# Weight loads beside attention's first loads, a one-piece softmax for the third half sequence, and new ranks for the first stage

## The chip, the cores and the metric

The kernel runs on one core of one Trainium2 chip. The metric is the device time of one execution in microseconds (us); the time before is the median of three runs. All rows of traces come from one profiled execution of the kernel before.

## What is computed

Eight batches of windowed attention over eight heads (576 positions, 64 wide), the heads side by side as rows of a 4608 x 512 matrix, and a feed-forward layer with an exact gelu on it, in float32:

```
scores = q @ k.T / 8
scores = where(mask, scores, -1e9)   # heads 0-3: the last 32 keys
                                     # heads 4-7: every 4th of the last 128 keys
attn = exp(scores - max(scores))
attn = attn / (sum(attn) + 1e-9)
x = (attn @ v) rearranged to [4608, 512]
h = x @ w_in                         # 512 -> 2048
g = 0.5 * h * (1 + erf(h / sqrt(2)))
out = g @ w_out                      # 2048 -> 512
```

The two weight matrices come as float64 (the kernel gets them as pairs of 32-bit words and makes a high and a low float32r part of each number).

## The kernel before

The 4608 rows are cut into 16 half sequences of 288 rows, `c` = 0 to 15. Attention of one half sequence is done for four pairs of heads, `p` = 0 to 3: pairs 0 and 1 have the plain window (96 rows in use), pairs 2 and 3 the dilated one (128 rows). "(1,3)" below is half sequence 1, pair 3.

For each pair `load` (L271) fetches queries and keys, `load_v` (L280) the values, `scores` (L302) multiplies queries and keys on PE, `lowest` (L318) adds the mask and finds the lowest of the negated scores on DVE, in three steps of two instructions, `softmax` (L331) takes the exponential on ACT, in three steps of two instructions of 64 columns each, with the row's lowest as bias and the row's sum as a second result. `norm` (L338) divides by the sum (two small DVE instructions and one multiplication of 128 x 384), `turn` (L351) transposes, `av` (L363) multiplies with the values on PE, and `xout` splits the product into a high part (ACT) and a low part (DVE), `xh` and `xl`.

The feed-forward layer runs over 16 blocks `f` of the hidden dimension. `ffn_h` (L410) makes 12 matmuls of 128 x 288 for one block and half sequence, then the gelu and a cast on ACT and a subtraction on DVE (L426). `ffn_o` (L428) makes 12 matmuls per block for the output. Each block needs the weights `win[f]` and `wouts[f]`. A weight block of 128 x 512 float64 numbers is fetched by `w_load` (L193), one transfer of 512 KB, and split by `w_rest` and `w_low`: six DVE instructions of 128 x 512 (L241, L243, L203, L205, L209, L253) and one cast on ACT. Block 0 of `w_in` takes another way, `w_join` and `w_join_pe`, with three matmuls on PE.

There are two stages. In the second, the half sequences 2 to 15 go one after the other in an order written by hand (from L573 on): feed-forward of `c`, with the attention of `c + 1` put between its matmuls. The first stage does everything else: all 32 weight blocks, attention of half sequences 0, 1 and 2, and the feed-forward layer of 0 and 1. Here a planner (`Plan`, L49) sets the order. Each piece of work is a job with costs in us, a list of jobs that it follows, buffers that it takes and gives back, and a rank. The planner keeps a clock per engine, and takes at each step the job that could start first, with a small weight of the rank (`KAPPA`); the constants at L39 to L46 are its margins and ranks. Its result is only the order in which instructions stand in each engine's queue: on the chip each engine works through its queue in order and waits at an instruction whose inputs are not there.

What matters for the change: SP issues all transfers, in its own order. `weight_jobs` (L508) starts the first weight load only after the last of the query/key loads of half sequence 0 has begun, and lets at most five weight blocks be loaded ahead of the splitting. Gelu and exponential need different tables of ACT, so all exponentials of half sequence 1 come before the first gelu, and those of half sequence 2 behind the last gelu of half sequence 1 (`gate`, L534). The values of half sequence 2 use the buffer of half sequence 1's `x` parts, and are loaded once that is free. Output blocks `d` = 2 and 3 of half sequence 1 are left for the end of the first stage (96 matmuls), to give PE work while the third softmax runs. Below, h(c,f) is `ffn_h` of half sequence `c` and block `f`; h(2,0) is the first work of the second stage.

Of the kernel before, what the change touches and what calls it, by code (L numbers as in the profile page):

```python
# [12 lines left out]
ALU = mybir.AluOpType  # L13
# [24 lines left out]

LATE, LATE_PE, COLD = 0.25, 0.2, 45  # L39
KAPPA, AHEAD, N_PE = 5.4e-05, 5, 1  # L40
R_ATT, R_P = (0, 340, 260), -12
R_F = 220
R_A = {"load": 152, "v": -162, "scores": -118,
       "exp": 52, "norm": 28, "t": -206, "av": 2, "x": -288, "low": -58}
R_W, R_WL = -76, 1092
R_H, R_O, R_E, R_O1 = 1088, 976, 780, 544  # L46

# [84 lines left out]
def attn_ffn(ctx: ExitStack, tc: tile.TileContext, qk_p, qk_d, v_p, v_d, w_in, w_out, outT):  # L132
# [60 lines left out]
    def w_load(s, src, dst, i):  # L193
        yield {"DMA": 1.6}
        s["raw"] = wo.tile([P, DM, 2], U32, tag="wo", name="raw_w")
        nc.sync.dma_start(s["raw"], src.bitcast(U32).rearrange("p (n t) -> p n t", t=2))
# [167 lines left out]
    def av(s, banks=None):  # L364

        yield {"PE": (0.9 if s.plain else 1.2) if s.c < 2 else 0.9}
        n = NU * s.nq
# [105 lines left out]
    def attention_jobs(plan, c, prev, gate):  # L473

        for p in range(NPAIR):
# [19 lines left out]
            def all_of(name, n):  # L495
                return [(name,) + k] + [(name, u) + k for u in range(n - 1)]
            add("scores", scores(s), [("load",) + k] + [("scores",) + j for j in last], ["m", "m"], [ring])
            chained("low", NU, lowest, lambda b: [("scores",) + k], ["sm"], ["m", "m"])
            chained("exp", NU, softmax, lambda b: [all_of("low", NU)[0] if b == NU - 1 else ("low", b) + k] + gate)
            add("norm", norm(s), all_of("exp", NU))  # L500
            add("t", turn(s), [("norm",) + k], ["sm"], ["sm"])
            own = ["px"] if c < 2 else ["m", "m"]
            add("av", av(s), [("t",) + k, v], own, ["sm"] + ([ring] if c < 2 else []))
            add("x", xout(s), [("av",) + k] + ([("x1",)] if c == 1 else [("h", 0, NF - 1)] if c == 2 else []), give=own)
# [3 lines left out]
    def weight_jobs(plan, i):  # L508
# [6 lines left out]
        def add(name, gen, after, take=(), give=(), delay=0.15):  # L515
            plan.add((name, i), gen, after, take, give, rank + (R_WL if name == "wload" else 0), delay)
        chain = ([("begun", ("wload", i - 1))] if i else [("begun", ("load", 0, NPAIR - 1))])
        if i >= AHEAD:
# [14 lines left out]
    k = attention_jobs(plan, 1, k, [])  # L533
    attention_jobs(plan, 2, k, [("h", 1, NF - 1)])  # L534
    plan.add(("units",), w_units(), take=["go"], rank=R_W)
    for i in range(2 * NF):
# [9 lines left out]
    for f in range(NF):  # L546
        rank = R_W + R_F * f
        for c, gs in ((0, g0), (1, g1)):
            plan.add(("h", c, f), ffn_h(xs[c], f, gs), [("x", c, p) for p in range(NPAIR)] +
                     [("wlow", 2 * f), ("whigh", 2 * f)] + [("exp", 1, p) for p in range(NPAIR)] +  # L550
                     ([("begun", ("h", c, f - 1))] if f else []),
# [133 lines left out]
```

## Time and profile before

| | us |
|---|---|
| median of three runs | 969.88 |
| the runs | 967.44, 969.88, 969.89 |
| the profiled execution | 969.69 |
| its span, first to last instruction | 967.9 |
| PE busy / DVE busy / ACT busy in the span | 931.8 / 486.4 / 439.0 |
| h(0,0) starts on PE | 50.62 |
| h(2,0) starts on PE | 173.96 |

The span is cut by stages. From 0 to 40 us the transfers run at 89% of what 16 DMA engines can be busy, and PE is busy for 16 us of 40. From 40 to 141 us DVE is busy without a gap, mostly with the splitting of weights. From 141 to 174 us the first stage ends, and from 174 us on PE is busy all the time, in equal pieces of 56.9 us per half sequence. A busy share over the whole span (PE 96%) says little here; the stages have to be read one by one.

### The profile page before, as it was taken

To read this page: it belongs to the slowest core of one execution; us is meant where nothing else is said; L and a number is where in the kernel's file an instruction comes from. 1 tells how busy PE (TensorE), PEld (TensorE's weight loads), DVE (VectorE), ACT (ScalarE), POOL (GpSimd) and SP (SyncE) were. 2 spreads that over 40 slices of the span, in tenths; PEclk is the share of its full clock that TensorE was granted. 3 is DMA by queue.
4 is the path that set the end of the run, shared out by engine and by line. 5 is a ranking of instruction groups with operands and counts; after the bars stand their busy time and mean duration, and the time that the engine had idled before them with its cause. 6 is when DMAs were issued, how large, how long until landed. Compare 5 with 4: busy or idle time off the path is not lost.

```text
span 967.9 us, 27863 instructions
## 1 busy us (share of the span) xinstructions
PE 931.8 (96%) x11860; PEld 910.6 (94%) x11860; DVE 486.4 (50%) x1796; ACT 439.0 (45%) x1420; POOL 5.6 (1%) x27
## 2 busy tenths in 40 slices
PE   3689989999999999999999999999999999999998
PEld 3489988999999999999999999999999999999998
DVE  4699996353354535335353533536353363624420
ACT  5445445462634546263454625345362544536240
POOL 2000000000000000000000000000000000000000
PEclk9999999999999999999999999999999999999999
DMA  9633323304021130402203040220404022040000
GB/s 304 247 132 105 114 88 109 130 8 142 2 87 64 46 104 8 142 2 78 73 26 124 8 142 2 78 72 14 136 7 140 4 77 73 8 142 8 20 1 25
DMA packets 32252, 74.80 MB, mean 77 GB/s; under 512 B 3584, under 2 KB 11776, under 8 KB 32128
## 3 DMA queue, kind: packets, MB, share of 16 engines
q1 hardware_dynamic: 32128, 73.02, 22.8%
q8 instruction: 93, 1.52, 0.7%
q14 instruction: 31, 0.25, 0.1%
HBM read 63.57 MB, written 9.44 MB: 75 GB/s over the span
## 4 chain that ended last, share of the span: by engine, by line
PE 86%; DVE 9%; DMA 3%; issue 1%; ACT 0%; SPq 0%; DVEq 0%
PE ps_o L431 39%; PE ps_h L417 38%; PE px_a L386 4%; PE ps_a L315 3%; DVE cv L205 2%; DVE raw_w L243 2%; DMA raw_qk<-qk_p 1%; PE px L386 1%; DVE g L426 1%; DVE raw_w L209 1%; DVE cv L203 1%; DVE win L253 1%; DVE wout L253 1%; DVE raw_w L241 1%; DMA raw_qk<-qk_d 1%
## 5 line engine op out<-in xcount | busy, mean ns | idle before, releaser
L431 PE MATMUL ps_o<-g,wout 128*128 128x288 f32 x3072 | 425.3, 297 | 2.4 <-DVE g L426 1.4
L431 PEld LDWEIGHTS ps_o<-g,wout 128*128 128x128 f32 x3072 | 412.9, 189 | 4.9 <-DVE g L426 2.3
L417 PE MATMUL ps_h<-xh,win 128*128 128x288 f32 x1920 | 391.1, 298 | 3.0 <-DVE win L253 1.7
L417 PEld LDWEIGHTS ps_h<-xh,win 128*128 128x128 f32 x1920 | 309.0, 188 | 6.8 <-DVE win L253 2.5
L417 PE MATMUL ps_h<-xl,win 128*128 128x288 f32 x960 | 283.4, 295 | 0.0
L426 DVE TENSOR_TENSOR g<-gf,g 128x288 fp32r<-128x288 f32 x256 | 117.1, 458 | 260.2 <-ACT g L424 260.1
L421 ACT ACTIVATE gf<-ps_h 128x288 f32<-128x288 f32 x256 | 105.2, 411 | 299.6 <-PE ps_h L417 298.8
L417 PEld LDWEIGHTS ps_h<-xl,win 128*128 128x128 f32 x960 | 181.5, 189 | 0.0
L335 ACT ACTIVATE sm<-sm,st 128x64 f32<-128x64 f32 (+1 forms) x384 | 127.8, 334 | 11.3 <-DVE st L327 11.1
L424 ACT CAST g<-gf 128x288 fp32r<-128x288 f32 x256 | 110.9, 433 | 7.8
L404 ACT CAST xh<-px_a 128x288 fp32r<-128x288 f32 x52 | 28.0, 539 | 140.7 <-PE px_a L386 112.1
L362 DVE STREAM_TRANSPOSE turned<-sm 32x192 f32<-32x192 f32 x196 | 72.4, 369 | 5.2
L335 ACT ACTIVATION_READ_ACCUMULATOR sm<-sm,st 128x1 f32 (+1 forms) x384 | 71.8, 187 | 0.0
L181 DVE COPY o_sb<-ps_o 128x288 f32<-128x288 f32 x61 | 27.7, 455 | 86.7 <-PE ps_o L431 82.2
L406 DVE TENSOR_TENSOR xl<-px_a,xh 128x288 fp32r<-128x288 f32 x52 | 29.6, 569 | 58.4 <-ACT xh L404 58.0
L327 DVE CUSTOM_DVE_ANT_0 sm<-ps_a,masks 96x64 f32<-96x64 f32 (+1 forms) x312 | 46.9, 217 | 0.0
L386 PEld LDWEIGHTS px_a<-turned,v_all 64*64 64x64 f32 x2184 | 38.6, 134 | 4.2 <-issue 4.2
L386 PE MATMUL px_a<-turned,v_all 64*64 64x24 f32 (+1 forms) x2184 | 41.4, 218 | 0.0
L357 DVE STREAM_TRANSPOSE turned<-sm 96x384 f32<-96x384 f32 (+1 forms) x64 | 36.8, 575 | 3.8 <-PE px L386 1.9
L349 DVE TENSOR_TENSOR sm<-sm,st 96x384 f32<-96x384 f32 (+1 forms) x63 | 34.9, 555 | 2.0
L327 DVE DVE_READ_ACCUMULATOR2_ANT st<- 128x1 f32 (+1 forms) x384 | 31.0, 81 | 0.0
L340 DVE TENSOR_SCALAR st<-st 96x6 f32<-96x6 f32 (+1 forms) x64 | 10.4, 164 | 39.6 <-ACT sm L335 38.7
(46 smaller groups left out, 374.4 us busy)
## 6 DMA issues: line engine op xcount, KB each, us to landing
raw_qk<-qk_d SPq DMA_DIRECT2D x32, 368.0 KB, 5.5
v_all<-v_p SPq DMA_DIRECT2D x28, 384.0 KB, 4.1
v_all<-v_d SPq DMA_DIRECT2D x28, 384.0 KB, 5.4
raw_qk<-qk_p SPq DMA_DIRECT2D x32, 304.0 KB, 3.5
outT<-o_sb SPq DMA_DIRECT2D x64, 144.0 KB, 1.8
raw_w<-w_in SPq DMA_DIRECT2D x16, 512.0 KB, 3.6
raw_w<-w_out SPq DMA_DIRECT2D x16, 512.0 KB, 4.4
v_sb<-v_d SPq DMA_DIRECT2D x4, 384.0 KB, 8.7
```

Of the source, the lines that this page charges most:

```text
L327: nc.vector.tensor_tensor_reduce(out=s.sm[0:s.rows, i], in0=s.sc[h][0:s.rows, cols], in1=mask_of(s, u), scale=-SCALE, scalar=3.0e38, op0=A ...
L335: nc.scalar.activation(t, t, AF.Exp, bias=s.st[0:s.rows, 0, i:i + 1], scale=-1.0, accum_out=s.st[0:s.rows, 1, i:i + 1])
L349: nc.vector.tensor_mul(t, t, s.st[0:s.rows, 2].unsqueeze(2).broadcast_to((s.rows, 2 * NU, 2 * KB)))
L357: nc.vector.transpose(s.t[0:s.rows].rearrange("p i j b -> p (i j b)"), s.sm[0:s.rows].rearrange("p i k -> p (i k)"))
L362: nc.vector.transpose(s.t[32 * to:32 * to + 32, :, r % 2], s.sm[32 * r:32 * r + 32, :, j * KB:(j + 1) * KB])
L386: nc.tensor.matmul(px[h * D:(h + 1) * D, r - r0, u * s.nq:(u + 1) * s.nq], s.v[rows, u, j, h * D:(h + 1) * D], s.t[rows, 2 * u + h, j, 0:s ...
L406: nc.vector.tensor_sub(l, px, h)
L417: nc.tensor.matmul(ps, wins[f][:, t, cc * P:(cc + 1) * P], xx, start=(n == 0), stop=(n == 3 * NC - 1))
L421: nc.scalar.activation(gf, ps, AF.Gelu)
L424: nc.scalar.copy(g[:, 0], gf)
L426: nc.vector.tensor_sub(g[:, 1], gf, g[:, 0])
L431: nc.tensor.matmul(ps, wouts[f][:, t, d * P:(d + 1) * P], gs[f][:, u], start=(f == 0 and n == 0), stop=(f == NF - 1 and n == 2))
```

## The change

Four things are changed.

1. The first weight load follows the first query/key load of half sequence 0, not the last of the four.
2. For half sequence 2 the softmax of a pair is done in one piece: `less` subtracts the rows' lowest on DVE (one instruction of 128 x 384), `wide` takes one exponential of 384 columns on ACT instead of six of 64, and `sums` adds up the rows on DVE (one instruction). `less` stands ahead of the last gelu of half sequence 1, `wide` and `sums` behind it.
3. All ranks, margins and some costs of the planner are set anew, and its jobs `scores` and `av` get longer delays.
4. The job `units` (two small DVE instructions that `w_join_pe` needs) follows the exponentials of pair (0,1). The new constant `GATE` has the value that the code had before.

```diff
-LATE, LATE_PE, COLD = 0.25, 0.2, 45
-KAPPA, AHEAD, N_PE = 5.4e-05, 5, 1
-R_ATT, R_P = (0, 340, 260), -12
-R_F = 220
-R_A = {"load": 152, "v": -162, "scores": -118,
-       "exp": 52, "norm": 28, "t": -206, "av": 2, "x": -288, "low": -58}
-R_W, R_WL = -76, 1092
-R_H, R_O, R_E, R_O1 = 1088, 976, 780, 544
+LATE, LATE_PE, COLD = 0.3, 0.7, 38
+KAPPA, AHEAD, N_PE = 2e-05, 5, 1
+R_ATT, R_P = (0, 670, 480), 92
+R_F = 324
+R_A = {"load": 156, "v": -142, "scores": 58,
+       "exp": 32, "norm": 104, "t": -154, "av": -202, "x": -280, "less": -116, "sums": -72, "low": -106}
+R_W, R_WL = -448, -324
+R_H, R_O, R_E, R_O1 = 856, 1160, 1048, 644
...
+    def wide(s):
+
+        yield {"ACT/exp": 0.46}
+        t = s.sm[0:s.rows]
+        nc.scalar.activation(t, t, AF.Exp, scale=-1.0)
+
+    def less(s):
+        yield {"DVE": 0.47}
+        t = s.sm[0:s.rows]
+        nc.vector.tensor_sub(t, t, s.st[0:s.rows, 0].unsqueeze(2).broadcast_to((s.rows, 2 * NU, 2 * KB)))
+
+    def sums(s):
+        yield {"DVE": 0.47}
+        nc.vector.tensor_reduce(s.st[0:s.rows, 1], s.sm[0:s.rows], axis=mybir.AxisListType.X, op=ALU.add)
...
-            chained("exp", NU, softmax, lambda b: [all_of("low", NU)[0] if b == NU - 1 else ("low", b) + k] + gate)
-            add("norm", norm(s), all_of("exp", NU))
+            if c < 2:
+                chained("exp", NU, softmax, lambda b: [all_of("low", NU)[0] if b == NU - 1 else ("low", b) + k] + gate)
+                add("norm", norm(s), all_of("exp", NU))
+            else:
+                add("less", less(s), all_of("low", NU))
+                add("exp", wide(s), [("less",) + k] + gate)
+                add("sums", sums(s), [("exp",) + k])
+                add("norm", norm(s), [("sums",) + k])
...
-        chain = ([("begun", ("wload", i - 1))] if i else [("begun", ("load", 0, NPAIR - 1))])
+        chain = [("begun", ("wload", i - 1))] if i else [("begun", ("load", 0, 0))]
...
-    plan.add(("units",), w_units(), take=["go"], rank=R_W)
+    plan.add(("units",), w_units(), [("exp", 0, 1)], ["go"], rank=R_W)
```

What the planner makes of it is seen in the queues. SP's queue, from its start: `raw_qk` are queries and keys, `v_sb` values, `raw_w` weights; `_p` is plain, `_d` dilated. Before:

```order
L278 DMA raw_qk<-qk_p 128x608
L285 DMA v_sb<-v_p 96x768
L278 DMA raw_qk<-qk_p 128x608
L285 DMA v_sb<-v_p 96x768
L278 DMA raw_qk<-qk_d 128x736
L285 DMA v_sb<-v_d 128x768
L278 DMA raw_qk<-qk_d 128x736
L285 DMA v_sb<-v_d 128x768
```

And with the change:

```order
L280 DMA raw_qk<-qk_p 128x608
L198 DMA raw_w<-w_in 128x1024
L287 DMA v_sb<-v_p 96x768
L280 DMA raw_qk<-qk_p 128x608
L287 DMA v_sb<-v_p 96x768
L280 DMA raw_qk<-qk_d 128x736
L287 DMA v_sb<-v_d 128x768
L198 DMA raw_w<-w_out 128x1024
L198 DMA raw_w<-w_in 128x1024
L280 DMA raw_qk<-qk_d 128x736
L287 DMA v_sb<-v_d 128x768
L198 DMA raw_w<-w_out 128x1024
```

Before, the first weight load is the 21st transfer, behind 16 transfers of half sequences 0 and 1 and the four query/key loads of half sequence 2. Now it is the second; weights are transfers 2, 8, 9, 12, 13 and 20, the last query/key load of half sequence 1 is transfer 21 (it was 15), and the query/key loads of half sequence 2 are 22, 23, 25 and 28. Between 24 and 30 stand four more weight loads.

PE's queue up to h(0,0): `ps_sc` are scores, `px` the products with the values (x36 a plain pair, x48 a dilated one), `ps_w` the join of the first weight block, `ps_h` h(c,f). Before:

```order
L315 MATMUL ps_sc<-raw_qk 32x64 x36
L386 MATMUL px<-turned,v_sb 64x24 x48
L315 MATMUL ps_sc<-raw_qk 32x64 x24
L386 MATMUL px<-turned,v_sb 64x32 x36
L231 MATMUL ps_w<-cv,ident 128x512
L232 MATMUL ps_w<-win_148,units 128x512
L233 MATMUL ps_w<-gw,units 128x512
L386 MATMUL px<-turned,v_sb 64x24 x48
L315 MATMUL ps_sc<-raw_qk 32x64 x24
L417 MATMUL ps_h<-xh,win_148 128x288 x2
```

And with the change:

```order
L317 MATMUL ps_sc<-raw_qk 32x64 x60
L403 MATMUL px<-turned,v_sb 64x32 x36
L233 MATMUL ps_w<-cv,ident 128x512
L234 MATMUL ps_w<-win_148,units 128x512
L235 MATMUL ps_w<-gw,units 128x512
L317 MATMUL ps_sc<-raw_qk 32x64 x24
L403 MATMUL px<-turned,v_sb 64x32 x36
L317 MATMUL ps_sc<-raw_qk 32x64 x36
L403 MATMUL px<-turned,v_sb 64x24 x48
```

The join of the first weight block moves from behind six products with values to behind one, and h(0,0) follows after five products and ten of the twelve score groups (it was seven and all twelve). Two score groups and three products now stand behind h(0,0); before, one product did.

ACT's queue at the end of the first stage: gelu (`gf`), cast (`g`), output copies (`o_sb`), the exponentials of half sequence 2 (`sm`) and the high parts of `x`. Before:

```order
L421 ACTIVATE gf<-ps_h 128x288
L424 CAST g<-gf 128x288
L179 COPY o_sb<-ps_o 128x288
L335 ACT_TABLE_LOAD
L335 ACTIVATE sm,st<-sm,st 128x64 x12
L335 ACTIVATE sm,st<-sm,st 96x64 x12
L404 CAST xh<-px_2361 128x2x72
```

And with the change:

```order
L438 ACTIVATE gf<-ps_h 128x288
L441 CAST g<-gf 128x288
L181 COPY o_sb<-ps_o 128x288 x2
L344 ACT_TABLE_LOAD
L344 ACTIVATE sm<-sm 96x384 x2
L344 ACTIVATE sm<-sm 128x384 x2
L181 COPY o_sb<-ps_o 128x288 x3
L421 CAST xh<-px_2367 128x3x64
```

Twenty-four exponentials become four, and the plain pairs now come first, there and in the products with values that follow on PE.

## Rows read from the trace of the kernel before

**Rows 1.** The page: the span, and the busy time of each engine.

```profile
span 967.9 us, 27863 instructions
...
PE 931.8 (96%) x11860; PEld 910.6 (94%) x11860; DVE 486.4 (50%) x1796; ACT 439.0 (45%) x1420; POOL 5.6 (1%) x27
```

**Rows 2.** Busy us by stage: PE, PEld, DVE, ACT, POOL, clock, DMA share, GB/s.

```profile
0.00:40.00 40.00, 16.01 (x760) 13.60 (x762) 18.71 (x132) 19.75 (x101) 5.57 (x27) 1.00 0.89 305
40.00:141.00 101.00, 94.41 (x1031) 88.73 (x1030) 100.90 (x264) 46.13 (x101) 0.00 (x0) 1.00 0.37 116
141.00:174.00 33.00, 30.53 (x342) 29.46 (x343) 21.86 (x57) 15.96 (x66) 0.00 (x0) 0.90 0.26 81
174.00:231.00 57.00, 57.00 (x722) 56.09 (x722) 25.38 (x101) 28.00 (x88) 0.00 (x0) 1.00 0.26 88
```

**Rows 3.** The same for DVE alone, up to its last weight instruction.

```profile
0.00:147.30 147.30, 125.71 (x406) 0.99 0.49 163
```

**Rows 4.** SP's timeline: the first weight load.

```profile
18.58 0.33 SPq L196 DMA_DIRECT2D raw_w<-w_in  x1
```

**Rows 5.** PE's timeline: start, us, line, tiles, count, idle before it.

```profile
12.35 0.67 PE L315 MATMUL ps_sc<-raw_qk 64*32 64x64 f32 x29
16.34 1.19 PE L315 MATMUL ps_sc<-raw_qk 64*32 64x64 f32 x55 [3.33 <-issue]
...
23.07 1.73 PE L315 MATMUL ps_sc<-raw_qk 64*32 64x64 f32 x84 [4.09 <-DMA raw_qk<-qk_d]
...
29.50 1.07 PE L386 MATMUL px<-turned,v_sb 32*64 32x24 f32 x55 [3.90 <-issue]
...
39.26 0.64 PE L315 MATMUL ps_sc<-raw_qk 64*32 64x64 f32 x17 [1.17 <-issue]
...
50.62 0.85 PE L417 MATMUL ps_h<-xh,win 128*128 128x288 f32 x2 [0.32 <-issue]
```

**Rows 6.** The page, DMA queues: kind, packets, MB, share of 16 engines.

```profile
q8 instruction: 93, 1.52, 0.7%
```

**Rows 7.** The chain of waits, second stage: matmuls of `ffn_h` and `ffn_o` in a row.

```profile
192.35 9.80 PE ps_h L417 x72
202.15 10.74 PE ps_o L431 x81
```

**Rows 8.** The chain of waits, first stage: steps of the weight splitting on DVE.

```profile
52.05 0.60 DVE raw_w L243
...
53.25 0.34 DVE cv L203
```

**Rows 9.** Who PE waited for, 50 to 175 us: first and last of eight.

```profile
PE ps_h L417 <- DVE win L253: 1.7, 2, 1.0
...
PE ps_h L417 <- issue: 0.3, 1, 0.3
```

**Rows 10.** PE in two stretches: busy us (instructions), granted clock, DMA share, GB/s.

```profile
144.00:146.00 2.00, 2.00 (x11) 0.53 0.00 0
...
164.00:166.00 2.00, 2.00 (x10) 0.50 0.22 74
```

**Rows 11.** PE's timeline at the end of the first stage.

```profile
149.61 9.68 PE L431 MATMUL ps_o<-g,wout 128*128 128x288 f32 x72
160.96 1.26 PE L386 MATMUL px<-turned,v_all 64*64 64x24 f32 x48 [1.68 <-DMA v_all<-v_d]
...
173.96 0.43 PE L417 MATMUL ps_h<-xh,win 128*128 128x288 f32 x2
```

**Rows 12.** DVE's timeline there: an output copy that waits for an output transfer.

```profile
153.63 0.46 DVE L181 COPY o_sb<-ps_o 128x288 f32<-128x288 f32 x1 [1.72 <-DMA outT<-o_sb]
```

**Rows 13.** ACT by line, 150 to 174 us: the exponentials of half sequence 2.

```profile
L335 ACT ACTIVATE sm<-sm,st 128x64 f32<-128x64 f32 (+1 forms) x24 | 8.0, 334 | 0.0
```

**Rows 14.** Engines by line, 0 to 174 us: DVE's multiplication by 1/sum; ACT's gelu.

```profile
L349 DVE TENSOR_TENSOR sm<-sm,st 96x384 f32<-96x384 f32 (+1 forms) x11 | 6.0, 550 | 0.2
...
L421 ACT ACTIVATE gf<-ps_h 128x288 f32<-128x288 f32 x32 | 13.2, 412 | 39.0 <-PE ps_h L417 39.0
```

More of the change, by code (lines that the diff above doesn't have):

```diff
@@ L118 @@
 N_EARLY = 2
+GATE = NF - 1
 def at_once(gen):
@@ L193, in w_load @@
     def w_load(s, src, dst, i):
-        yield {"DMA": 1.6}
+        yield {"DMA": 1.4}
         s["raw"] = wo.tile([P, DM, 2], U32, tag="wo", name="raw_w")
@@ L302, in scores @@
     def scores(s, banks=None):
-        yield {"PE": 0.6}
+        yield {"PE": 0.75}
         if banks is None:
@@ L364, in av @@
     def av(s, banks=None):
-        yield {"PE": (0.9 if s.plain else 1.2) if s.c < 2 else 0.9}
+        yield {"PE": (1.2 if s.plain else 1.6) if s.c < 2 else 0.9}
         n = NU * s.nq
@@ L496, in all_of @@
                 return [(name,) + k] + [(name, u) + k for u in range(n - 1)]
-            add("scores", scores(s), [("load",) + k] + [("scores",) + j for j in last], ["m", "m"], [ring])
+            add("scores", scores(s), [("load",) + k] + [("scores",) + j for j in last], ["m", "m"], [ring], 1.5)
             chained("low", NU, lowest, lambda b: [("scores",) + k], ["sm"], ["m", "m"])
-            chained("exp", NU, softmax, lambda b: [all_of("low", NU)[0] if b == NU - 1 else ("low", b) + k] + gate)
-            add("norm", norm(s), all_of("exp", NU))
+            if c < 2:
[6 more added lines that the diff above has]
+                add("norm", norm(s), [("sums",) + k])
             add("t", turn(s), [("norm",) + k], ["sm"], ["sm"])
             own = ["px"] if c < 2 else ["m", "m"]
-            add("av", av(s), [("t",) + k, v], own, ["sm"] + ([ring] if c < 2 else []))
+            add("av", av(s), [("t",) + k, v], own, ["sm"] + ([ring] if c < 2 else []), 1.5 if c < 2 else 0.3)
             add("x", xout(s), [("av",) + k] + ([("x1",)] if c == 1 else [("h", 0, NF - 1)] if c == 2 else []), give=own)
@@ L533, in attn_ffn @@
     k = attention_jobs(plan, 1, k, [])
-    attention_jobs(plan, 2, k, [("h", 1, NF - 1)])
-    plan.add(("units",), w_units(), take=["go"], rank=R_W)
+    attention_jobs(plan, 2, k, [("h", 1, GATE)] if GATE >= 0 else [])
+    plan.add(("units",), w_units(), [("exp", 0, 1)], ["go"], rank=R_W)
     for i in range(2 * NF):
@@ L549, in attn_ffn @@
             plan.add(("h", c, f), ffn_h(xs[c], f, gs), [("x", c, p) for p in range(NPAIR)] +
-                     [("wlow", 2 * f), ("whigh", 2 * f)] + [("exp", 1, p) for p in range(NPAIR)] +
+                     [("wlow", 2 * f), ("whigh", 2 * f)] + [("exp", c2, p) for c2 in range(1, 2 + (GATE == -1)) for p in range(NPAIR)] +
                      ([("begun", ("h", c, f - 1))] if f else []),
```

## The prediction

> **What bounds the kernel now.** I read the busy times by stage first. From 174 us on PE is busy without a gap [rows 2], in a part that the change leaves as it is. So one moment decides: the start of h(2,0) on PE, at 173.96 [rows 11]. From there to the end of the span are 967.9 - 173.96 = 793.9 us [rows 1], and the execution's own time, 969.69, is 1.8 above its span. The forecast is the new start of h(2,0) plus 795.7. (The profiled execution lies 0.2 us below the median of 969.88.)
>
> Three things limit the first stage in turn. Up to 40 us the transfers do: they are 89% busy and PE works 16 us of 40 [rows 2]. DVE works only 18.7 of these 40 us; up to its last weight instruction at 147.3 it is busy for 125.7 [rows 3], so 21.6 us are idle, 21.3 of them before 40. The first weight load is issued at 18.58 only [rows 4], so there is nothing to split. From 40 to 141 DVE is full [rows 2] and PE waits for it now and then. Then comes the third softmax, in which PE stops for 1.68 us [rows 11].
>
> PE's timeline shows a limit that the busy times hide. PE stops inside groups of matmuls, where no input can be missing: after 29 of the score matmuls at 12.35, and after the stop at 16.34 it does 55 + 72 = 127 matmuls to the next stop, which ends at 23.07; another ends at 29.50 [rows 5]. A refill of PE's instructions explains the number: queue q8 moved 1.52 MB in 93 packets, 16.3 KB each [rows 6]; PE's 11860 + 11860 instructions [rows 1] make that 64 bytes each, so a packet holds 256 instructions, 128 matmuls with their weight loads. The refills take some 6.5 us each while transfers are dense (16.34, 23.07, 29.50), and the fifth ends at 39.26 [rows 5].
>
> **The change, part by part.**
>
> *PE up to h(0,0).* Counted as the timeline counts (scores 36 a plain pair, 48 a dilated one; products 72 and 96), 1108 matmuls stand ahead of h(0,0) before, 820 now. The first 221 need no refill, each later one brings 127. So h(0,0) was in the seventh refill and is now in the fifth, 91 matmuls behind its start. With refills as before, that is 39.26 + 91 x 0.02 (84 take 1.73 [rows 5]) = 41.1. The transfers are as dense as before: 6.7 MB of attention and ten weight loads (5.1 MB) are issued up to the 30th transfer now, and the first 30 before hold the same. But weights ahead of queries make PE reach the point where it asks for the second refill later: DVE's queue has the first step of weight block 1 (transfer 8; 2.96 MB at 305 GB/s [rows 2], some 10 to 13 us) ahead of the lowest of pair (0,2), and 6 us of work from there to the transposed pair (0,1), so the product of (0,1) starts at 19 to 20 instead of 17.5. I add 1.9: h(0,0) at 43.0, where it was at 50.62 [rows 5]. Bounds: with no refill to wait for it is bound by data, 8.67 MB up to the query/key load of (2,1), 28.4 us at 305 GB/s, then scores, softmax and product: 37.5. If the refills take longer: see the rivals.
>
> *PE from h(0,0) to h(2,0).* 384 matmuls of `ffn_h` at 9.80/72 = 0.136 and 384 of `ffn_o` at 10.74/81 = 0.1326 [rows 7] are 52.3 + 50.9. The four products of half sequence 2 (168 matmuls at 1.07/55 = 0.0195 [rows 5]) are 3.3. Moved behind h(0,0) are two score groups (2.0) and two products more than before (three, 264 matmuls, 5.1; before one, 1.4). Now 113.6, before 107.9. So of the 7.6 us that h(0,0) gains, 5.7 are given back: moved work is not saved work.
>
> *Lost time in that stretch.* Before it took 173.96 - 50.62 = 123.3, so 15.4 were lost. Piece by piece:
> - The first h runs at half rate, 0.85 for two matmuls against 0.43 later [rows 5, 11]: 1.6. It stays.
> - PE's waits, eight rows with 7.7 in all [rows 9], 6.0 without the one in the softmax. Nearly all are for DVE's weight splitting. I take 1.5, for this reason. DVE's work up to its last weight instruction is 125.7 + 4 x 0.55 for `less` (priced as the multiplication of the same shape [rows 14]) - 0.55, since one multiplication more goes to ACT: 127.4. The instructions ahead of its first subtraction of g, at 0.34 and 0.60 from start to start for the splitting [rows 8], sum to 39; that subtraction follows h(0,0) (43.0 + 3.2 at half rate), gelu and cast (1.2), so it stands at 47.4 and DVE has idled 8.4 by then. I see no later input that must come late, so the last weight instruction ends at 127.4 + 8.4 = 135.8, not 147.3. PE gets to the matmuls that need it at 43.0 + 1.6 + 92 = 137: PE is now a little behind DVE, where it was ahead.
> - Half clock after a wait, 11 instead of 15 matmuls in 2 us at 0.53 [rows 10]: 1.0 around 144. It goes with the waits.
> - The end: from the end of h(1,15), 149.61, to h(2,0) are 24.35 [rows 11]; PE's work there is 126 x 0.1326 + 3.3 = 20.0; lost 4.4, half of it in the stretch at clock 0.50 behind the stop [rows 10].
> - The rest, 2.4, stays.
>
> *The end with the new softmax.* ACT's 24 exponentials, one every 0.33 us, took 8.0 [rows 13]. Four of 384 columns cost, going on from 334 ns at 64 columns [rows 13] to 412 at 288 [rows 14], about 0.45 each, 1.8 together; bounds 0.41 and 6 x 0.334 = 2.0. So ACT is done 6 us sooner, and DVE is late next. Ahead of its sums stand two output copies, of which the second waits for an output transfer as one does before (1.72 [rows 12]); some 5.3 us after h(1,15) it starts the first sum. Up to the first transposed pair it then has four sums (2.2), eight small instructions (1.4), three multiplications (1.65) and four transposes (1.5): 12 us after h(1,15). PE gets there after 81 matmuls, 10.7. Stop: 1.3, and about 1.0 more at the third product. I take 2.3 lost instead of 4.4. A sum's price has no row; a subtraction's 0.55 is the nearest, none and 1.1 the bounds, which move the end by -1.3 to +2.2.
>
> *Sum.* Lost now 1.6 + 1.5 + 2.3 + 2.4 = 7.8. h(2,0) at 43.0 + 113.6 + 7.8 = 164.4, 9.6 earlier: 164.4 + 795.7 = **960.1**.
>
> **A rule against a row.** The rows show stops that end with a refill [rows 5, 6]. The Trainium skill, "Runtime: NRT & Kernel Launch", section "Instruction fetch mechanics", says that instructions come in blocks of 16 KiB, and that crossing a block is mostly hidden. The size agrees with the packets here; that it is hidden does not, while transfers are dense. By that rule the stops would have another cause, and the first rival below follows.
>
> **The rivals.**
> - *Data alone sets h(0,0).* For it: PE's stop before 23.07 is put down to a transfer [rows 5]. Against: the stops inside groups, 127 matmuls apart. Then h(0,0) is at 37.5, h(2,0) at 158.9: 954.6.
> - *PE's waits are not reduced.* The queues are in order, and new neighbours can make new waits: DVE waits for a weight in a transfer that SP holds back, or for g. For it: PE and DVE are within 2 us of each other over 90 us. With 15.4 lost as before h(2,0) is at 172.0: 967.7, no change.
> - *Early weights help nobody.* DVE's queue now begins with a weight instruction; were attention held up as much as splitting gains, h(0,0) would stay at 50 and h(2,0) come at 171.4: 967.1. Against: DVE has 21 idle us to give.
> - *Slower: refills take longer.* One mechanism: the transfers that wait ahead of a refill are now partly of 512 KB, and a refill waits its turn among them. If one takes 10 us instead of 6.5, the fifth ends at 16.3 + 4 x 10 = 56.3, h(0,0) is at 60 and h(2,0) at 181.4: 977.1. It decides from h(0,0) at 52.6 on, where h(2,0) is back at 174.0. Against: weight loads alone were under way when the stop before 29.50 ended, 6.4 after the one before it [rows 5]. The Trainium skill, "DMA: Bandwidth & Descriptors", section "Queues, rings and completion order", has each DMA engine take turns between its queues, packet by packet; by that rule a refill doesn't wait for the whole of what is queued, and this rival falls.
>
> **How the numbers follow.** Forecast 0.57, data alone 0.15, waits not reduced 0.13, early weights useless 0.05, slower 0.10. The forecast's own range is 956 to 965 (h(0,0) 41 to 46, the sums' bounds). The range reaches to 952 (data alone, with less lost at the end) and to 967.8 (waits not reduced), and leaves out the slower case and little else. About 0.3%, 2.9 us, is what a measurement of this kernel can tell from no change. Faster than 967.0 are the first two cases and a third or so of the next two: 0.78; slower than 972.8 is the last: 0.10; between them 0.12.
>
> **What will show it.** Right: h(0,0) at 41 to 46 on PE, with four or five stops 127 matmuls apart ahead of it; DVE idle for 8 to 10 us in all up to its last weight instruction, which ends near 136; waits of PE on weights at 1 to 3 us; no stretch at half clock around 140; four exponentials under 0.6 us each; 21.5 to 23 us from h(1,15) to h(2,0); h(2,0) at 163 to 166, and 56.9 us per half sequence from there. Wrong: h(0,0) before 40 (refills were not it) or after 50; or h(0,0) as forecast, and h(2,0) later than 168, which means that new waits ate the gain; or a change behind h(2,0).

## The result, and the profile after

Four runs of the changed kernel have a median of 960.03 us (958.96 to 960.91), the kernel before beside them 969.74: a ratio of 0.9905, 95% interval 0.9886 to 0.9924, so about 1% faster. The forecast was 960.1. The profiled execution took 960.52 us.

The page after, span and busy times (before: [rows 1]):

```profile
span 958.7 us, 27831 instructions
...
PE 926.3 (97%) x11860; PEld 906.8 (95%) x11860; DVE 486.9 (51%) x1800; ACT 435.0 (45%) x1385; POOL 6.2 (1%) x27
```

Busy time by stage, columns as in [rows 2]:

```profile
0.00:40.00 40.00, 17.14 (x712) 13.26 (x712) 26.83 (x148) 20.33 (x97) 6.20 (x27) 0.75 0.97 330
...
130.00:165.00 35.00, 35.00 (x403) 34.20 (x403) 27.88 (x71) 14.50 (x34) 0.00 (x0) 1.00 0.28 92
```

DVE alone up to its last weight instruction (before: [rows 3]):

```profile
0.00:141.50 141.50, 125.51 (x408) 0.88 0.52 169
```

In the first 40 us DVE works 26.8 us instead of 18.7, and the DMA share rises from 0.89 to 0.97. Up to its last weight instruction DVE does the same 125.5 us of work but idles 16.0 us instead of 21.6, so it ends near 141.5 instead of 147.3. From 130 to 165 PE does not stop.

PE's timeline (before: [rows 5, 11]):

```profile
17.50 0.43 PE L317 MATMUL ps_sc<-raw_qk 64*32 64x64 f32 x24 [0.45 <-issue]
...
26.89 1.12 PE L317 MATMUL ps_sc<-raw_qk 64*32 64x64 f32 x41 [4.82 <-issue]
...
33.52 0.43 PE L403 MATMUL px<-turned,v_sb 32*64 32x24 f32 x10 [4.08 <-issue]
...
37.76 1.34 PE L403 MATMUL px<-turned,v_sb 32*64 32x24 f32 x77 [1.61 <-issue]
...
42.45 0.66 PE L317 MATMUL ps_sc<-raw_qk 64*32 64x64 f32 x23 [1.76 <-issue]
...
44.49 0.85 PE L434 MATMUL ps_h<-xh,win 128*128 128x288 f32 x2
...
56.70 0.26 PE L317 MATMUL ps_sc<-raw_qk 64*32 64x64 f32 x1 [2.89 <-issue]
56.89 0.85 PE L434 MATMUL ps_h<-xh,win 128*128 128x288 f32 x2
...
144.09 10.87 PE L448 MATMUL ps_o<-g,wout 128*128 128x288 f32 x81
...
164.86 0.42 PE L434 MATMUL ps_h<-xh,win 128*128 128x288 f32 x2
```

The stops ahead of h(0,0) still fall inside groups of matmuls, 127 apart (10 + 96 + 19 is 125, 77 + 49 is 126). The first ends at 17.50, the fifth at 42.45, and h(0,0) starts at 44.49 instead of 50.62. One more stands at 56.70, 382 (three times 127, and one) matmuls behind the fifth. During this last stop the DMA engines were 8% busy (columns: from and to, length, PE busy, clock, DMA share, GB/s), so a stop does not need dense transfers beside it:

```profile
53.80:56.70 2.90, 0.01 (x1) 0.52 0.08 30
```

From the end of h(1,15), at 144.09, to h(2,0) are 20.8 us instead of 24.35, without a stop. The 793.8 us behind h(2,0) are as before.

Who PE waited for from 40 to 170 us; the refills are under "issue" (before, the eight rows of [rows 9]):

```profile
PE ps_sc L317 <- issue: 4.7, 2, 2.9
PE px L403 <- PE ps_h L434: 0.8, 1, 0.8
PE ps_o L448 <- DVE g L443: 0.8, 1, 0.8
```

The new softmax, ACT and DVE by line from 140 to 165 us (before: [rows 13]):

```profile
L344 ACT ACTIVATE sm<-sm 96x384 f32<-96x384 f32 (+1 forms) x4 | 1.8, 513 | 0.0
...
L353 DVE TENSOR_REDUCE st<-sm 96x6 f32<-96x384 f32 (+1 forms) x4 | 2.1, 542 | 0.2 <-ACT sm L344 0.2
```

DVE's timeline, the output copy ahead of the sums (before: [rows 12]):

```profile
147.40 0.46 DVE L183 COPY o_sb<-ps_o 128x288 f32<-128x288 f32 x1 [1.38 <-DMA outT<-o_sb]
```

Four exponentials take 1.8 us where 24 took 8.0; a sum costs 0.54, and the row that the forecast took as the nearest says 0.55.

### The profile page after: what moved, and what is told of

Read it like the earlier page. It is cut to its first block, busy times and chain, and to the rows that moved or that the text cites. A ratio compares the mean times of both kernels' runs of the same rounds, so it can differ in the third digit from the quotient of the medians.

```text
span 958.7 us, 27831 instructions
## 1 busy us (share of the span) xinstructions
PE 926.3 (97%) x11860; PEld 906.8 (95%) x11860; DVE 486.9 (51%) x1800; ACT 435.0 (45%) x1385; POOL 6.2 (1%) x27
## 4 chain that ended last, share of the span: by engine, by line
PE 89%; DVE 7%; issue 2%; DMA 2%; SPq 0%; ACT 0%
PE ps_o L448 40%; PE ps_h L434 40%; PE px_a L403 4%; PE ps_a L317 3%; DVE cv L207 1%; DVE raw_w L245 1%; PE px L403 1%; DMA raw_qk<-qk_p 1%; DVE g L443 1%; DMA raw_qk<-qk_d 1%; PE ps_sc L317 1%; DVE raw_w L243 1%; DVE wout L255 1%; DVE cv L205 1%; DVE raw_w L211 1%
## 5 line engine op out<-in xcount | busy, mean ns | idle before, releaser
L443 DVE TENSOR_TENSOR g<-gf,g 128x288 fp32r<-128x288 f32 x256 | 116.9, 457 | 261.5 <-ACT g L441 261.5
L337 ACT ACTIVATE sm<-sm,st 96x64 f32<-96x64 f32 (+1 forms) x360 | 119.9, 334 | 14.4 <-DVE st L329 14.2
L337 ACT ACTIVATION_READ_ACCUMULATOR sm<-sm,st 96x1 f32 (+1 forms) x360 | 67.4, 187 | 0.0
L423 DVE TENSOR_TENSOR xl<-px_a,xh 128x288 fp32r<-128x288 f32 x52 | 29.4, 565 | 58.5 <-ACT xh L421 58.1
L329 DVE DVE_READ_ACCUMULATOR2_ANT st<- 96x1 f32 (+1 forms) x384 | 30.9, 81 | 0.0
L317 PE MATMUL ps_sc<-raw_qk 64*32 64x64 f32 x504 | 11.3, 285 | 20.2 <-issue 9.9
```

Source lines behind the costliest of these rows:

```text
L317: nc.tensor.matmul(s.sc[h][32 * r:32 * r + 32, u * 2 * KB:(u + 1) * 2 * KB], x[:, q0:q0 + 32], x[:, k0:k0 + 2 * KB], start=True, stop=True)
L329: nc.vector.tensor_tensor_reduce(out=s.sm[0:s.rows, i], in0=s.sc[h][0:s.rows, cols], in1=mask_of(s, u), scale=-SCALE, scalar=3.0e38, op0=A ...
L443: nc.vector.tensor_sub(g[:, 1], gf, g[:, 0])
```

## The experiments

Each kernel is the changed one with one edit, unless said otherwise. The ratio is to the kernel before on the same chip; h(0,0), "split" (the end of DVE's last weight instruction), h(1,15) (its end) and h(2,0) are in us of the profiled execution. Long lines of the edits are shortened to the part that changes. Where the order moved `ffn_o` matmuls of the tail ahead of the end of h(1,15), that end is later by them alone: 12 in late_again (1.6 us), 6 in all_first and few_first (0.8), 3 in wide_alone (0.4).

| run | h(0,0) | split | h(1,15) | h(2,0) | ratio (95%) |
|---|---|---|---|---|---|
| before | 50.6 | 147.3 | 149.6 | 174.0 | 1 |
| after | 44.5 | 141.6 | 144.1 | 164.9 | 0.9905 (0.9886 to 0.9924) |
| after_again | 45.3 | 141.1 | 143.6 | 164.4 | 0.9905 (0.9881 to 0.9929) |
| all_first | 58.1 | 137.5 | 147.4 | 168.7 | 0.9962 (0.9951 to 0.9972) |
| few_first | 39.6 | 138.6 | 154.6 | 175.2 | 1.0026 (1.0015 to 1.0037) |
| two_later | 44.7 | 138.5 | 146.8 | 167.6 | 0.9936 (0.9915 to 0.9956) |
| late_again | 44.5 | 142.8 | 146.7 | 165.9 | 0.9938 (0.9916 to 0.9960) |
| more_dve | 43.5 | 152.7 | 154.3 | 175.1 | 1.0022 (1.0011 to 1.0033) |
| less_dve | 44.0 | 137.4 | 141.1 | 161.9 | 0.9897 (0.9880 to 0.9915) |
| pieces_again | 45.0 | 140.5 | 146.2 | 169.9 | 0.9960 (0.9948 to 0.9972) |
| wide_alone | 52.3 | 149.7 | 150.6 | 172.1 | 0.9994 (0.9984 to 1.0003) |
| pool_less | 43.7 | 139.7 | 145.5 | 166.3 | 0.9942 (0.9925 to 0.9959) |
| pool_g | 42.4 | 150.8 | 156.3 | 178.0 | 1.0105 (1.0060 to 1.0149) |

**The control.**

> The changed kernel as it is, for comparison on the same chip with the three others and, through the kernel before, with the first four: ratio to the kernel before 0.989 to 0.992, h(0,0) at 44 to 45, h(2,0) at 164 to 166.

It repeats the result. h(0,0) is 0.3 later than expected and 0.8 later than in the first profile, yet h(2,0) is 0.4 earlier: two profiles of one kernel differ by this much, so a single difference below 1 us says little.

**What stands ahead of h(0,0): all_first.**

```diff
-[("load",) + k] + [("scores",) + j for j in last]
+[("load",) + k] + [("scores",) + j for j in last] + (([("begun", ("t", 1, 3))] if p > 1 else []) if c == 2 else [])
...
-                     ([("begun", ("h", c, f - 1))] if f else []),
+                     ([("begun", ("h", c, f - 1))] if f else [("av", 1, 2), ("scores", 2, 3)]),
```

> The changed kernel with the first ffn_h held back until all scores of half sequence 2 and the products up to (1,2) are issued: 1179 matmuls ahead of h(0,0) instead of 819, as before the change and a little more; transfers in the same order, early weights as they are, and not one instruction more. Refill theory: the 1179th matmul is in the eighth refill, three later than now (42.45); at 4.2 to 6.6 us each h(0,0) starts at 57 to 64, the moved work saves 7.2 us behind it and the stop at 56.7 with its half clock (some 4.5) goes, so h(2,0) comes at 166 to 171 and the time is 961 to 966. Rival (early weights, DVE's head start, are the gain; refills only follow): h(0,0) at 44.5 + 7.2 = 51.7, h(2,0) as now, time 960 or a little less.

Time (964.86) and h(0,0) (58.06) are as the refill theory said, but the mechanism is only half of it. Up to 40.88 the stops are the same refills. The next three stand at the borders of groups and are not 127 apart. PE's timeline:

```profile
46.58 1.52 PE L403 MATMUL px<-turned,v_sb 32*64 32x32 f32 x72 [3.25 <-issue]
50.91 1.57 PE L403 MATMUL px<-turned,v_sb 32*64 32x24 f32 x96 [2.81 <-issue]
...
56.55 1.57 PE L403 MATMUL px<-turned,v_sb 32*64 32x24 f32 x96 [2.50 <-issue]
```

And DVE's:

```profile
46.03 0.44 DVE L423 TENSOR_TENSOR x<-px,x 128x288 fp32r<-128x288 f32 x1
50.40 0.41 DVE L423 TENSOR_TENSOR x<-px,x 128x288 fp32r<-128x288 f32 x1
55.80 0.65 DVE L423 TENSOR_TENSOR x<-px,x 128x288 fp32r<-128x288 f32 x1
```

Each product starts 0.10 to 0.11 us after DVE has subtracted the high part of x from the one `px` tile (46.47, 50.81, 56.45), which frees it for the next. So products one behind another wait 8.6 us for DVE, whose queue is full of weight splitting; `ffn_h` between them hide that wait. From h(0,0) to the end of h(1,15) PE is then busy all the time (89.4 of 89.4 us). With all early weights kept and DVE done 4.1 us sooner than in the changed kernel, PE ends h(1,15) 3.4 us later. Against the kernel before, h(2,0) is 5.3 us earlier, 3.1 of them in the tail (2.3 with as many matmuls in it): without PE's new order all the rest of the change, DVE's head start among it, carries 2 to 3 of the change's 9.1 ahead of the tail.

**Fewer ahead of h(0,0): few_first.**

```diff
-[("load",) + k] + [("scores",) + j for j in last]
+[("load",) + k] + [("scores",) + j for j in last] + ([("begun", ("h", 0, 2 * p))] if c == 2 else [])
-[("t",) + k, v]
+[("t",) + k, v] + ([("begun", ("h", 0, p))] if k[0] == 1 else [])
```

> The changed kernel with less ahead of h(0,0): the scores of half sequence 2 and the first product of half sequence 1 are moved behind it, one group between two ffn_h each; 675 matmuls ahead instead of 819, nothing else added or left out. Refill theory: the 675th is in the fourth refill (37.76 now), 73 behind its start, so h(0,0) at 39 to 40.5; no stop behind a run of small matmuls at 56.7, since ffn_h stand between them; 2.9 us of moved work are given back; h(2,0) at 158 to 163, time 954 to 958. Rival (data set h(0,0) now): h(0,0) stays at 43 or later, and the time is 959 to 961.

The first half came out: 675 matmuls ahead, h(0,0) in the fourth refill, at 39.55. The second half is a miss by over 12 us. PE's longest waits from 40 to 160 us:

```profile
PE px L403 <- DVE x L423: 3.8, 1, 3.8
PE px L403 <- issue: 2.8, 1, 2.8
PE ps_h L434 <- DVE st L329: 1.9, 1, 1.9
PE ps_o L448 <- DVE g L443: 1.3, 3, 0.7
```

Against the changed kernel that is 3.8 + 1.9 more of waits for DVE, whose lowest values and subtractions now stand behind weights that PE does not need yet (DVE has split the last at 138.6, 16 us before PE ends h(1,15)). And `ffn_h` begins at half rate (0.85 us for two matmuls) at 39.55, 46.06, 53.57 and 65.87, in the changed kernel at 44.49 and 56.89 only; one such group of 12 takes 3.1 us, at full rate 1.7. A start 5 us earlier was worth nothing: PE came to the following work before its inputs.

**The stop at 56.70: two_later.**

```diff
-[("load",) + k] + [("scores",) + j for j in last]
+[("load",) + k] + [("scores",) + j for j in last] + (([("begun", ("h", 0, 2 * p - 1))] if p > 1 else []) if c == 2 else [])
```

> The changed kernel with two score groups of half sequence 2 (those of its third and fourth pair, 96 matmuls) moved from between the first three ffn_h to later places, between ffn_h and ffn_o; 819 matmuls ahead of h(0,0) as now. Refill theory: h(0,0) at 44.5 as now, no stop behind a run of small matmuls at 56.7, and no half clock behind it, so up to 4.5 us less: h(2,0) at 160.5 to 163, time 956 to 958.5. Rival (DVE, full from 45 on, bounds this stretch; PE's stop at 56.7 is time that it would otherwise wait for split weights): waits of PE on DVE grow by as much, h(2,0) at 164 to 166, time 959 to 961.

The stop went (so it hung on the run of small matmuls), and DVE finished 2.6 to 3.1 us sooner, but h(1,15) ended 2.7 to 3.2 us later, for waits like these, of its PE from 40 to 185 us:

```profile
PE ps_h L434 <- DVE st L329: 2.3, 1, 2.3
...
PE px L403 <- DVE x L423: 1.1, 1, 1.1
```

The first is `ffn_h` waiting for a bank that late scores hold until DVE has their lowest values. It is the rival's side, and beyond it: h(2,0) at 167.6 and a median of 962.31, where the rival said at most 166 and 961. What PE gains at the stop it waits out elsewhere.

**A refill with nothing else to transfer: refill_idle.**

```diff
+    idle = [ps_m.tile([P, 512], F32, tag="m", name="ps_i") for _ in range(2)]
+    for n in range(256):
+        h = n % 2
+        nc.tensor.matmul(idle[h][0:32, 0:64], ident[h * D:(h + 1) * D, 0:32], ident[h * D:(h + 1) * D, 0:64],
+                         start=True, stop=True)
```

> The changed kernel with 256 more small matmuls (fp32, 64 rows by 64 columns, as the scores; results unused) at its very end, 512 as the timeline counts, where no transfer but the last outputs is under way. It prices a refill with the queues empty. Theory of the prediction (refills are slow because transfers are dense): PE still stops every 127 matmuls, but a refill takes under 4 us from one to the next, 1.7 to 2.5 of which are work. Rival (a refill of this length costs what it costs, whatever the queues hold): 4.2 to 6.6 us from one to the next, as at 25 to 45 us now.

```profile
954.59 14.48 PE L651 MATMUL ps_i<-ident 64*32 64x64 f32 x512
```

PE's timeline shows one row without a stop, and the instruction queue moved 97 packets, four more than [rows 6], as 1024 instructions in packets of 256 should. These matmuls took 0.028 us each, the scores 0.014 to 0.026, so 127 of them last 3.6 us: with idle queues a refill takes at most that. The expected stops did not show, so this one execution bounds the price and does not measure it. From stop to stop ahead of h(0,0) in the changed kernel are 9.4 us (17.50 to 26.89, with two shorter waits, 1.2 and 0.9, in it) and then 6.6, 4.2 and 4.7, the last three at DMA shares of 1.03, 1.00 and 0.82. The share alone does not explain 6.6 against 4.2, nor the 2.89 at 56.70 at a share of 0.08; that stays open.

**Early weights: late_again.**

```diff
-R_W, R_WL = -448, -324
+R_W, R_WL = -400, -324
-        chain = [("begun", ("wload", i - 1))] if i else [("begun", ("load", 0, 0))]
+        chain = [("begun", ("wload", i - 1))] if i else [("begun", ("load", 0, NPAIR - 1))]
```

> The changed kernel with the first weight load waiting for the fourth pair's queries again (the weights' rank at -400 instead of -448, since the planner finds no order at -448): the first weight is transfer 8 instead of 2, five weights instead of seven among the first 18 transfers, still before its place in the old kernel (21); 819 matmuls ahead of h(0,0) as now. Refill theory: h(0,0) within 1.5 us of 44.5; DVE's work of the first 45 us can still mostly be done before 45; time 959 to 962. Rival (the early weights are the gain): DVE falls behind by what it does not do early, 4 to 7 us of waits of PE for split weights, time 964 to 967.

h(0,0) is at 44.51 and the fifth stop ends at 42.49 (42.45 now); h(2,0) is 1.1 to 1.5 us later in the profile, and the ratio's interval just overlaps the control's. DVE had done 32.3 us of work by 45 us (31.8 in the changed kernel), so weights from 4 us on serve it as well as from 1 us on. The edit of the chain by itself, in the kernel before with its old ranks, leaves the program the same, instruction for instruction. It is the ranks that bring the loads forward.

This run also says more of the stop behind h(0,0). The 382nd matmul behind the fifth stop is here the second of an `ffn_h`, and PE stops there:

```profile
56.23 0.61 PE L434 MATMUL ps_h<-xh,win 128*128 128x288 f32 x1 [2.40 <-issue]
```

So the count sets the place of a stop, and the small matmuls ahead of it whether it shows (two_later).

**Who bounds the middle: more_dve and less_dve.**

```diff
         nc.vector.tensor_scalar(s["raw"][:, :, 1], s["f"], 0xFF800000, None, op0=ALU.bitwise_and)
+        nc.vector.tensor_scalar(s["raw"][:, :, 1], s["f"], 0xFF800000, None, op0=ALU.bitwise_and)
```

> The changed kernel with one instruction of each weight block's splitting done twice (0.34 us on DVE, 32 times, 10.9 us; the result is the same), nothing moved. If DVE bounds the stretch from 45 to 141 us, as the forecast said that it is within 2 us of PE: about 2.4 of it (the first seven blocks) fall into DVE's early idle time, 2.8 more into its idle time behind 45, and the rest, 5.7, shows: h(2,0) 4 to 8 us later, time 964 to 968. Rival (PE bounds that stretch and DVE has slack): h(2,0) at most 2 us later, time 960 to 962.

```diff
-        nc.vector.tensor_scalar(raw[:, :, 0], raw[:, :, 0], 9, None, op0=ALU.logical_shift_right)
```

> The changed kernel without the first instruction of the splitting's remainder in 31 of 32 weight blocks (the shift by 9 of the low words, 0.34 us on DVE, 10.5 us in all; the low parts of the weights come out wrong, every later instruction stays). It is the reverse of the doubled instruction, which cost 11 us. Theory (DVE and PE are both near their bounds in the stretch up to h(1,15), DVE by 2 to 3 us the later one): h(2,0) 1 to 4 us earlier, at 161 to 164, time 956 to 959.5, with PE busy without a gap and DVE idle instead. Rival (DVE alone bounds the stretch): the full 9 to 10.5, time 949 to 951.

The doubled instruction (L211, L212) costs more than expected. DVE's timeline of more_dve, and its work up to its last weight instruction:

```profile
80.81 0.42 DVE L211 TENSOR_SCALAR raw_w<-cv 128x512 uint32<-128x512 uint32 x1
81.26 0.43 DVE L212 TENSOR_SCALAR raw_w<-cv 128x512 uint32<-128x512 uint32 x1
81.60 0.68 DVE L207 SCALAR_TENSOR_TENSOR cv<-raw_w,cv 128x512 uint32<-128x512 uint32 x1
...
0.00:152.73 152.73, 139.26 (x441) 0.89 0.47 157
```

From the first copy to the second are 0.45 us, to the next instruction 0.34 more. DVE's work is 139.3 us instead of 125.5, so 13.8 us were added and not 10.9. DVE's end and the median moved by 11.2 (152.73 against 141.56; 970.64 against 959.48), more than either theory said. DVE's idle time went from 16.0 to 13.5: 2.5 of the 13.8 fell into it, and 1.3 of these only because the first weight landed earlier in this profile (DVE waited 5.3 us for it, not 6.6).

Without the shift DVE's work is 116.9 us, 8.6 less (expected: 10.5). h(2,0) came 2.5 to 2.9 us earlier, as the theory said, but 0.5 to 1.3 of that is an earlier h(0,0), and the medians differ by 1.3 only (958.14 against 959.48, the ratios' intervals overlap). Two views of less_dve from 45 to 141 us, DVE's busy time and PE's (then clock, DMA share, GB/s):

```profile
45.00:141.00 96.00, 86.64 (x213) 0.98 0.33 105
...
45.00:141.00 96.00, 92.17 (x999) 0.98 0.33 105
```

DVE then idles 9.4 us. PE, which the theory had busy without a gap, keeps a stop of 3.2 us. So the two are near balance: more work on DVE shows nearly in full, and 8.6 us less of it give 1 to 3.

**The softmax by itself: pieces_again and wide_alone.**

```diff
-            if c < 2:
...
-                add("less", less(s), all_of("low", NU))
-                add("exp", wide(s), [("less",) + k] + gate)
-                add("sums", sums(s), [("exp",) + k])
-                add("norm", norm(s), [("sums",) + k])
...
+            add("norm", norm(s), all_of("exp", NU))
```

> The changed kernel with the third half sequence's softmax in six pieces a pair again (the subtraction and the sum on DVE gone, 24 exponentials on ACT). Theory of the prediction: ACT needs 8.0 us instead of 1.8 for the exponentials and the time from the end of h(1,15) to h(2,0) is back at 23.5 to 24.5 (20.8 now), h(0,0) unchanged at 44.5: time 962.5 to 964. Rival (the tail became shorter because the output copies stand elsewhere): tail 20.8 to 21.5, time 960 to 961.

As expected: 23.7 us from h(1,15) to h(2,0), time 963.98. Of the 5.0 to 5.5 us at h(2,0), 3.0 are in the tail; the others lie ahead of h(1,15), in the planner's new order (an `ffn_h` more at half rate, at 61.55, and a wait of 0.6 for a weight). PE's timeline there:

```profile
156.99 0.79 PE L403 MATMUL px<-turned,v_all 64*64 64x32 f32 x32 [1.29 <-DVE turned L379]
157.70 4.03 PE L448 MATMUL ps_o<-g,wout 128*128 128x288 f32 x18
```

Eighteen matmuls behind the stop take 4.03 us, where they take 2.4 at 0.133: half rate behind a wait, as in [rows 10].

The reverse, on the kernel before:

```diff
-       "exp": 52, "norm": 28, "t": -206, "av": 2, "x": -288, "low": -58}
+       "exp": 52, "norm": 28, "t": -206, "av": 2, "x": -288, "low": -58,
+       "less": 52, "sums": 28}
...
+                add("less", less(s), all_of("low", NU))
+                add("exp", wide(s), [("less",) + k] + gate)
+                add("sums", sums(s), [("exp",) + k])
+                add("norm", norm(s), [("sums",) + k])
```

> The kernel before with the third half sequence's softmax for a head pair at once, and its ranks, its weight loads' condition and their places as before (the two new steps get ranks between those of their neighbours). Theory of the prediction: from the end of h(1,15) to h(2,0) 21.5 to 23 instead of 24.35, nothing else; h(0,0) at 49.5 to 51; time 2 to 3 us below the kernel before. Rival (the third softmax is only worth something if DVE comes to it early): no difference.

The tail is 21.6 us, as expected (24.35 before), yet the median is only 0.6 us lower, with an interval of 1.6 lower to 0.3 higher. DVE up to its last weight instruction:

```profile
0.00:149.70 149.70, 128.10 (x411) 1.00 0.49 160
```

128.1 us of work instead of 125.7, idle 21.6 as before: the four subtractions `less` (0.55 each) run ahead of weight blocks in a full queue, whose last block comes 2.4 us later; h(1,15) ends 1.0 us later. (h(0,0) is at 52.3 here, outside the expected 49.5 to 51; whether h(1,15) is later for that or for DVE, this run does not tell.) Of the 2.8 that the tail gave, the profile keeps 1.8 and the medians 0.6.

**Off DVE: pool_less and pool_g.**

```diff
-        nc.vector.tensor_sub(t, t, s.st[0:s.rows, 0].unsqueeze(2)...)
+        nc.gpsimd.tensor_sub(t, t, s.st[0:s.rows, 0].unsqueeze(2)...)
```

> The changed kernel with the subtraction ahead of the third softmax's exponentials (four instructions of 0.55 us on DVE) on the idle GpSimd; it has some 90 us until ACT wants it. If DVE's 2.2 us in the middle are what the new softmax costs there (as the run with this softmax alone suggests): time 1 to 2.2 us less, 957 to 959. Rivals: the planner's new order, or GpSimd slowing DVE while both work, gives it back: 959.5 to 962.

DVE finished 1.4 to 1.9 us sooner, but in the planner's new order `ffn_h` starts at half rate four times (43.72, 49.25, 56.15, 60.84) instead of twice, and h(1,15) ended 1.4 us later: 962.31.

```diff
-        yield {"DVE": 0.37}
-        nc.vector.tensor_sub(g[:, 1], gf, g[:, 0])
+        e = yield {"POOL": 0.8} if x is xs[1] and f % 2 else {"DVE": 0.37}
+        (nc.gpsimd if e == "POOL" else nc.vector).tensor_sub(g[:, 1], gf, g[:, 0])
```

> The changed kernel with eight of the 32 subtractions that give the low part of g (0.37 us on DVE each, those of half sequence 1 in every second block, 3.0 us in all) on GpSimd. Theory as for the run with less DVE work: time 1 to 3 us less, 956.5 to 958.5. Rival: GpSimd is slower at it, PE waits for g where it waits for DVE now: 960 to 963.

It is the rival, and far worse than it said: 978.35. GpSimd's timeline:

```profile
68.63 14.90 POOL L443 TENSOR_TENSOR g<-gf,g 128x288 fp32r<-128x288 f32 x1 [59.93 <-ACT g L441]
88.49 0.80 POOL L443 TENSOR_TENSOR g<-gf,g 128x288 fp32r<-128x288 f32 x1 [4.96 <-ACT g L441]
```

And PE's:

```profile
83.58 0.61 PE L448 MATMUL ps_o<-g,wout 128*128 128x288 f32 x1 [8.55 <-POOL g L443]
```

PE waits 11.3 us for GpSimd, in two waits. None of the versions that compute the whole result is faster than the changed kernel.

## Why the prediction was right, and where it was not

By its own sum: h(2,0) = h(0,0) + the stretch to the end of h(1,15) + the tail. Forecast 43.0 + 99.1 + 22.3 = 164.4, measured 44.49 + 99.6 + 20.77 = 164.86. Three terms are off by 1.5, 0.5 and -1.5 us; that the total fits to 0.5 is partly their cancelling.

- *h(0,0).* Fifth refill and stops 127 apart came as forecast, and few_first moved h(0,0) into the fourth when its matmuls were moved. "Data alone" (37.5) is ruled out. Mis-sized by 1.5: the product of (0,1) started at 19.17, as assumed (19 to 20; 17.47 before), but the second stop then ended 7.7 us behind that start and not 5.6, so that the fifth ended 3.2 us later than before (42.45 against 39.26). Why the second stop ended so late is not shown.
- *"h(0,0) was in the seventh refill and is now in the fifth".* That is right as a count, but the seventh cost nothing to be seen. Before, the last stop ahead of h(0,0) was the sixth:

```profile
42.74 0.85 PE L315 MATMUL ps_sc<-raw_qk 64*32 64x64 f32 x35 [0.95 <-issue]
```

  It ended only 0.3 us later than the last stop now, and behind it came 7.9 us of work without a stop (251 small matmuls and the join of the first weight block), where now come 2.0 us (95 small matmuls). So 5.8 of the 6.1 us that h(0,0) gained are work that no longer stands there: the join now runs at 13.92, ahead of the stops, and two score groups and two products more come behind h(0,0).
- *Refills as the price of work ahead of h(0,0).* Too simple beyond the fifth: there the single `px` tile, freed by DVE, is late (all_first). The Trainium skill's rule that crossing a block is mostly hidden ("Runtime: NRT & Kernel Launch", "Instruction fetch mechanics") agrees with refill_idle, where no stop showed, and not with the four stops of 1.6 to 4.8 us ahead of h(0,0).
- *Work given back.* 113.6 us of PE work between h(0,0) and h(2,0) fits: measured 120.4, lost 6.8 (forecast 7.8).
- *The lost time.* PE's waits for DVE were 1.6, forecast 1.5: 0.8 for g, and 0.8 at 51.83, where the product starts 0.09 us after DVE has subtracted the high part of x from the `px` tile (51.74), as in all_first, though the view puts it down to `ffn_h`. The first h at half rate is there. Not foreseen: the refill stop at 56.70 (2.9) and the second `ffn_h` at half rate behind it (1.4), against a "rest" of 2.4. DVE then waits 2.5 us for g. Removing the stop did not bring its time in (two_later).
- *DVE's idle time.* The step that failed: forecast 8.4, measured 16.0, with 125.5 us of work where 127.4 were forecast. By its first subtraction of g, at 49.86 and not 47.4, DVE had done 36.7 us of work, not 39: idle 13.2; the wait for g behind the stop added 2.5. Its last weight instruction ended at 141.5, not 135.8. The sum had no term for stalls ahead of 45 us. Three show in DVE's own waits up to its last weight instruction: for the first weight itself (6.6), for a high part of x (2.2) and for scores (1.5), the last two behind PE's stops:

```profile
DVE cv L205 <- DMA raw_w<-w_in: 6.6, 1, 6.6
DVE g L443 <- ACT g L441: 2.9, 2, 2.5
DVE xl L423 <- ACT xh L421: 2.2, 1, 2.2
DVE sm L329 <- PE ps_sc L317: 1.7, 2, 1.5
```

- *PE behind DVE.* "PE is now a little behind DVE" holds for the last block: DVE had split it at 141.56, and PE came to its matmuls at 144.09 at the earliest (forecast 135.8 and 137). Both came later, so that DVE's delay hardly shows in PE's waits. But that is a balance and no room to spare: 13.8 us more on DVE cost 11.2, and 8.6 less gave 1 to 3 (more_dve, less_dve).

```profile
140.87 0.69 DVE L255 SCALAR_TENSOR_TENSOR wout<-raw_w 128x512 fp32r<-128x512 uint32 x1
```

- *The tail.* Exponentials (1.8) and sums (0.54) as priced. Forecast 2.3 lost, measured 0.8, so that the tail fell below the 21.5 to 23 that was to show it: the output copy waited 1.38 instead of 1.72, the first sum started 3.9 us after h(1,15), not 5.3, and PE never stopped, so the half rate behind a stop went too.
- *The rivals.* "Waits not reduced" fell (7.7 us to 1.6, refills apart). "Early weights help nobody" fell by its numbers (h(0,0) at 50, 967.1); what the early weights are worth is not shown, since no run with the new order has them late, late_again neither. "Refills take longer" fell as a whole: the last three took 4.2 to 6.6 us, the one before them 9.4. Credit for the change can't be split among its parts: the softmax alone is worth at most 1.6 us, the chain alone moves nothing, and with the new ranks the kernel without it is 4 to 5 us slower (963.98 against 959.48), of which 3.0 are the tail's. The ranks by themselves were not run.

## What to carry to other kernels

When two engines are within 3 us of each other over 100, a piece of work is worth what it costs on the engine that is late there: the wide softmax shortened the tail by 2.8 us and put 2.4 us of work on DVE, so by itself it gained little. Idle time at the start of a full engine's queue is little room for more work in the middle: 13.8 us added to DVE cost 11.2. An instruction that is added can cost more than its kind does elsewhere: the second copy came 0.45 us behind the first, and the next instruction 0.34 behind that. An earlier start for the next stage pays only if its inputs' queue moves with it; look at which small buffer's release sits behind long work.

## What the runs showed of the hardware

- One GpSimd subtraction of 128x288 took 0.80 us at best and 14.90 at worst; the four `less` on GpSimd took 1.15 to 3.68 us. In four cases of pool_g (14.90, 8.87, 7.28 and one of 3.22) DVE ran its instructions without gaps and at their usual pace until it had to wait for an input, and the subtraction ended 0.65 to 0.67 us after that moment. In three others, one of them in pool_less, DVE gave way instead: one instruction that takes 0.42 or 0.68 us elsewhere took 1.04, 1.06 and 1.18. GpSimd's and DVE's timelines (DVE ran out at 120.77 - 1.59 = 119.18, GpSimd ended at 119.83):

```profile
110.96 8.87 POOL L443 TENSOR_TENSOR g<-gf,g 128x288 fp32r<-128x288 f32 x1 [3.91 <-ACT g L441]
120.77 0.46 DVE L443 TENSOR_TENSOR g<-gf,g 128x288 fp32r<-128x288 f32 x1 [1.59 <-ACT g L441]
148.08 1.04 DVE L211 TENSOR_SCALAR raw_w<-cv 128x512 uint32<-128x512 uint32 x1
```

  The Trainium skill, "SBUF — State Buffer", section "SBUF: two separate sides", says that GpSimd shares a port pair with DVE as an exclusive lock, which the engine that starts first keeps for its whole instruction. These runs agree that one waits for the other, mostly GpSimd; that it is this port is not shown.
- `ffn_h` ran at half rate (0.85 us for two matmuls) when small matmuls and stops had gone before; one group of 12 costs 1.4 us more. In the kernel before, the profile's granted clock is 1.00 in the slice where h(0,0) takes 0.85 for two, so near the start of these traces the matmuls' own durations tell the clock better than that column:

```profile
48.00:52.00 4.00, 3.68 (x150) 1.00 0.40 116
```
